# Softmax reciprocals through 32x32 VectorE transposes, a reordered first batch, and four FFN groups a step ahead of the third batch

## The chip, the cores and the metric

The kernel runs on one core of one Trainium2 chip. The metric is device microseconds (us) of an execution. Engines are named as in the profile: PE is TensorE, PEld its weight loads, DVE is VectorE, ACT is ScalarE, POOL is GpSimd, SP is SyncE.

## The reference

Eight batches of eight heads: causal attention of 576 queries over 16 "beacon" keys and 576 keys, then a gated feed-forward network over all 4608 rows. Cut to what matters:

```python
k_all = np.concatenate([beacon_k, k], axis=2); v_all = np.concatenate([beacon_v, v], axis=2)
scores = scale * np.matmul(q, k_all.transpose(0, 1, 3, 2))        # 8 x 8 x 576 x 592
scores = np.where(causal, -1e9, scores); scores -= scores.max(-1, keepdims=True)
a = np.exp(scores); a /= a.sum(-1, keepdims=True) + 1e-09
x = (a @ v_all) -> rows of 512                                     # 4608 x 512
out = (np.maximum(x @ w_gate, 0) * (x @ w_val)) @ w_out            # d_ff = 1536
```

## The kernel before

Batches are counted from 0 in the code and as first, second, third in the text. A batch has two groups of four heads. The queries of a group are cut into three chunks of 240, 256 and 80 columns. Per chunk TensorE multiplies the exponentials `e` with the values (into PSUM tile `ab`) and with a 32-column block of ones (into `os`). So each of the 32 rows of a head's block in `os` holds the same sum. VectorE takes the reciprocal, multiplies, and records the least and the most reciprocal ("notes"), which say at the end whether the sums were in range.

```python
class Chunk:
    def av(self):
        # ... PSUM tiles self.ab [P, 2, 256] and self.os [P, 256] are taken
        cq0, _, segs = CHUNKS[self.ci]
        order = sorted(segs, key=lambda x: x[0])
        for i, (kt, q0, n, _, _) in enumerate(order):
            # ... for three parts (two of values, one of ones), for four heads:
                    nc.tensor.matmul(o[:, q0 - cq0:q0 - cq0 + n], w, e[...], ...)
    def invert(self):
        n = CHUNKS[self.ci][1]
        self.r = nrm.tile([P, 256], FP32, name="r")
        nc.vector.reciprocal(self.r[:, :n], self.os[:, :n])
    def scale(self):   # xT = ab * r, on VectorE
    def note(self):    # least = min(least, r); most = max(most, r), on VectorE
```

The program interleaves attention steps of one batch with FFN groups of the batches before it. A FFN "up" group is 8 matmuls of 512 columns, a "down" group 12. A plan says how many groups each step carries. VectorE also makes the FFN product `hT` of each up group.

```python
ALONE = ((0, 3, 3, 2), (3, 3))       # FFN groups between first and second, second and third batch
plan = ([(0, i, 0) for i in range(STEPS)] + [(None, 0, n) for n in ALONE[0]]
        + [(1, i, 1) for i in range(STEPS)] + [(None, 0, n) for n in ALONE[1]]
        + [(b, i, 3.0 if b == 2 else 4.4) for b in range(2, B) for i in range(STEPS)]
        + [(None, 0, 4.5)])
```

In the first batch, tiles of q and k are cast, transposed on TensorE and moved out of PSUM as they land. Weight loads (`wg`, `wv`), the casting loads of the second batch (`hwide`) and `wo` are issued in this order:

```python
after(1, lambda: load_w(wg, moe_w_gate, 0, 512))
after(2, lambda: load_w(wv, moe_w_val, 0, 512))
after(3, lambda: load_w(wg, moe_w_gate, 512, 1024))
after(4, lambda: load_w(wv, moe_w_val, 512, 1024))
after(6, lambda: load_w(wg, moe_w_gate, 1024, 1536))
after(6, lambda: load_w(wv, moe_w_val, 1024, 1536))
after(6, lambda: load_second(0))                # hwide
# ...
after(s2 - 1, lambda: load_wo(0, 6)); after(s2, lambda: load_wo(6, 12))
```

## Time and profile before

| | before |
|---|---|
| median of the first three runs | 391.03 us (390.27 to 391.34) |
| first FFN matmul | 27.80 us |
| first score matmul of the third batch | 82.5 us |
| batch period from the fourth batch on | 40.6 us |
| TensorE busy | 370.4 us, 95% |
| VectorE busy | 204.8 us, of which the largest group of reciprocals 61.0 us |

The page of the profile begins with busy times (first line below), and its part 5 lists groups of instructions: line, engine, operation, output and input tiles, count, then busy time and mean ns, then the engine's idle time just before them and who ended it.

```profile
PE 370.4 (95%) x4239; PEld 188.1 (48%) x4296; DVE 204.8 (52%) x333; ACT 191.9 (49%) x269; POOL 125.9 (32%) x217
...
PE 85%; DMA 6%; POOL 4%; issue 2%; DVE 1%; ACT 1%; SPq 0%; DVEq 0%
...
L393 DVE RECIPROCAL r<-os 128x240 f32<-128x240 f32 (+2 forms) x45 | 61.0, 1355 | 39.6 <-PE os L385 39.5
...
L385 PE MATMUL os<-e,ones 128*32 128x240 bf16 (+4 forms) x660 | 31.7, 230 | 0.0
```

TensorE is the bottleneck. The sum matmuls (`os<-e,ones`, last line) are never waited for: their idle time is 0.0. The reciprocals are long, but stand beside the path.

Where TensorE does lose time is at the third batch. In the windows table the column after POOL is PEclk, the clock granted to TensorE as a share of full speed; then come the DMA share and GB/s.

```profile
82.50:86.00 3.50, 0.58 (x13) 0.42 (x12) 0.69 (x1) 0.97 (x1) 0.58 (x1) 0.87 0.55 153
86.00:88.00 2.00, 2.00 (x9) 0.70 (x9) 0.00 (x0) 0.00 (x0) 0.00 (x0) 0.50 0.78 177
```

TensorE waits 2.92 us for a transposing DMA (`qT<-half`) near 83 us, and then runs at half clock until about 91.5 us.

From the fourth batch on all is full. Two timelines of one place, TensorE and then VectorE (start, duration, engine, line, operation, count, and in brackets idle time before it and its releaser):

```profile
165.69 0.39 PE L385 MATMUL ab<-e,v 128*32 128x240 bf16 x8
165.90 0.28 PE L385 MATMUL os<-e,ones 128*32 128x240 bf16 x4
```

```profile
165.32 0.69 DVE L430 TENSOR_TENSOR hT<-g,f 128x512 bf16<-128x512 f32 x1 [1.18 <-PE f L428]
165.93 0.40 DVE L405 TENSOR_TENSOR least<-least,r 128x240 f32<-128x240 f32 x1
166.25 0.40 DVE L405 TENSOR_TENSOR most<-most,r 128x240 f32<-128x240 f32 x1
166.56 1.65 DVE L393 RECIPROCAL r<-os 128x240 f32<-128x240 f32 x1
```

The sums start at 165.90 us, 0.21 us behind the value matmuls. VectorE is then in the FFN product (to 166.0) and in two notes (to 166.6). Only behind those comes the reciprocal. Nothing on TensorE waits for that queue.

### The profile page before, as it was taken

What the parts mean: (1) busy time and instruction counts of PE and PEld (TensorE: products, weight loads), DVE (VectorE), ACT (ScalarE), POOL (GpSimd) and SP (SyncE); (2) the same over time, 40 slices, a digit from 0 to 9 for tenths busy, and PEclk for the clock granted to TensorE, in tenths of its full rate; (3) what the DMA queues carried; (4) which work ended last, traced back from release to release, by engine and by line L of the source; (5) the groups of instructions that cost most, each with busy time, mean ns of one, the idle gap of its engine ahead of it and who ended that gap; (6) DMA issues with size and microseconds to landing.
All of it is one profiled execution on the core that took longest, in us unless ns stands there. A gap on an engine that the chain in (4) does not pass through costs nothing.

```text
span 390.5 us, 10175 instructions
## 1 busy us (share of the span) xinstructions
PE 370.4 (95%) x4239; PEld 188.1 (48%) x4296; DVE 204.8 (52%) x333; ACT 191.9 (49%) x269; POOL 125.9 (32%) x217
## 2 busy tenths in 40 slices
PE   7779999969999999999999999999999999999995
PEld 3554455424555545445544545454544554444443
DVE  4877477524674565466546653666365654512420
ACT  4763494225745654465446545655455533323321
POOL 1796455324632543254224332335201100000000
PEclk9999999987999999999999999999999999999999
DMA  7899999858966983687357834786200010011002
GB/s 227 186 176 195 206 187 215 180 149 199 186 140 182 190 169 85 165 187 147 82 160 183 177 85 131 170 190 90 97 29 2 2 76 33 2 40 71 0 27 88
DMA packets 146788, 49.85 MB, mean 128 GB/s; under 512 B 133296, under 2 KB 142256, under 8 KB 146736
## 3 DMA queue, kind: packets, MB, share of 16 engines
q1 hardware_dynamic: 137680, 43.37, 47.1%
q0 software_dynamic: 9056, 5.77, 10.5%
q8 instruction: 35, 0.57, 0.7%
q14 instruction: 17, 0.14, 0.1%
HBM read 38.27 MB, written 9.44 MB: 122 GB/s over the span
## 4 chain that ended last, share of the span: by engine, by line
PE 85%; DMA 6%; POOL 4%; issue 2%; DVE 1%; ACT 1%; SPq 0%; DVEq 0%
PE f L438 24%; PE f L419 22%; PE s L428 11%; PE f L428 11%; PE s L336 6%; PE ab L385 6%; DMA wo<-in_moe_w_out_dram 3%; PE os L385 2%; DMA raw<-in_v_dram 1%; POOL e L352 1%; DMA wide<-in_k_dram 1%; PE f L282 1%; POOL v L245 1%; POOL wg L312 1%; POOL wv L312 1%
## 5 line engine op out<-in xcount | busy, mean ns | idle before, releaser
L344 ACT ACTIVATE e<-s 128x1024 bf16<-128x1024 f32 (+2 forms) x112 | 104.3, 966 | 23.9 <-PE s L336 23.8
L419 PE MATMUL f<-xT,wg 128*128 128x512 bf16 x407 | 110.8, 385 | 1.5 <-DVE hT L430 0.3
L422 ACT ACTIVATE g<-f 128x512 f32<-128x512 f32 x108 | 64.6, 598 | 89.7 <-PE f L419 82.9
L438 PE MATMUL f<-wo,hT 128*128 128x512 bf16 (+1 forms) x420 | 94.8, 373 | 2.9 <-issue 1.6
L352 POOL TENSOR_SCALAR_AFFINE_SELECT e<-e 128x512 bf16<-128x512 bf16 (+2 forms) x80 | 47.3, 603 | 153.0 <-ACT e L344 145.7
L393 DVE RECIPROCAL r<-os 128x240 f32<-128x240 f32 (+2 forms) x45 | 61.0, 1355 | 39.6 <-PE os L385 39.5
L430 DVE TENSOR_TENSOR hT<-g,f 128x512 bf16<-128x512 f32 x54 | 37.1, 687 | 61.7 <-PE f L428 55.8
L430 DVE TENSOR_TENSOR hT<-g,s 128x512 bf16<-128x512 f32 x54 | 37.1, 687 | 60.2 <-PE s L428 57.1
L428 PEld LDWEIGHTS <-wv 128*128 128x128 bf16 x432 | 42.6, 99 | 53.2 <-issue 3.7
L438 PEld LDWEIGHTS <-hT 128*128 128x128 bf16 x444 | 41.4, 98 | 47.2 <-issue 0.8
L419 PEld LDWEIGHTS <-wg 128*128 128x128 bf16 x432 | 40.3, 99 | 48.3 <-issue 2.8
L441 ACT COPY ob<-f 128x512 f32<-128x512 f32 (+1 forms) x37 | 21.3, 575 | 72.5 <-PE f L438 72.5
L428 PE MATMUL s<-xT,wv 128*128 128x512 bf16 x213 | 56.0, 384 | 0.1
L428 PE MATMUL f<-xT,wv 128*128 128x512 bf16 x213 | 55.4, 380 | 0.6 <-ACT qT L283 0.2
L249 POOL CAST half<-raw 128x512 bf16<-128x512 f32 (+2 forms) x60 | 36.3, 621 | 22.8 <-DMA raw<-in_q_dram 9.9
L385 PE MATMUL ab<-e,v 128*32 128x80 bf16 (+4 forms) x1320 | 38.7, 231 | 2.0 <-POOL e L352 1.0
L336 PE MATMUL s<-qT,kT 64*128 64x80 bf16 (+3 forms) x704 | 34.7, 231 | 5.4 <-DMA qT<-half 2.9
L336 PEld LDWEIGHTS <-kT 64*128 64x128 bf16 x704 | 20.4, 96 | 28.7 <-issue 26.0
L385 PE MATMUL os<-e,ones 128*32 128x240 bf16 (+4 forms) x660 | 31.7, 230 | 0.0
L385 PEld LDWEIGHTS <-v 128*32 128x32 bf16 (+1 forms) x1408 | 26.4, 97 | 10.5 <-issue 5.3
L245 POOL CAST v<-raw 128x512 bf16<-128x512 f32 (+1 forms) x40 | 26.1, 657 | 12.4 <-DMA raw<-in_v_dram 12.1
L398 DVE TENSOR_TENSOR xT<-ab,r 128x480 bf16<-128x480 f32 (+2 forms) x45 | 25.0, 555 | 1.0
(59 smaller groups left out, 130.9 us busy)
## 6 DMA issues: line engine op xcount, KB each, us to landing
out_dram<-ob SPq DMA_DIRECT2D x35, 256.0 KB, 2.3
raw<-in_v_dram SPq DMA_DIRECT2D x24, 256.0 KB, 4.9
raw<-in_q_dram SPq DMA_DIRECT2D x24, 256.0 KB, 4.3
raw<-in_k_dram SPq DMA_DIRECT2D x18, 256.0 KB, 4.2
raw<-in_v_dram SPq DMA_DIRECT2D x8, 224.0 KB, 3.5
wg<-in_moe_w_gate_dram POOLq DMA_DIRECT2D x6, 256.0 KB, 5.9
wv<-in_moe_w_val_dram POOLq DMA_DIRECT2D x6, 256.0 KB, 6.6
wo<-in_moe_w_out_dram POOLq DMA_DIRECT2D x2, 768.0 KB, 10.5
```

Source lines behind the costliest of these rows:

```text
L245: copy(self.v[:n, t].rearrange("p (h a d) -> p h a d", a=2, d=C), raw[:n].rearrange("p (h d a) -> p h a d", a=2, d=C))
L249: copy(h[:n], raw[:n])
L336: nc.tensor.matmul(self.s[:, a, c + j * n:c + (j + 1) * n], self.batch.kT[rows, 2 * g + j, kt * P:(kt + 1) * P], self.batch.qT[rows, 2 * g ...
L344: nc.scalar.activation(e[:, :k * 4 * n].rearrange("p (k a x) -> p a k x", k=k, a=2), self.s[:, :, :k * 2 * n].rearrange("p a (k x) -> p a ...
L352: nc.gpsimd.affine_select(out=cols[:, :, :m], in_=cols[:, :, :m], pattern=[[0, 4], [1, m]], compare_op=ALU.is_ge, fill=0.0, base=base, cha ...
L385: nc.tensor.matmul(o[:, q0 - cq0:q0 - cq0 + n], w, e[:kr, 2 * (hh % 2) + hh // 2], start=(i == 0 and part != 1), stop=(i == self.last), sk ...
L393: nc.vector.reciprocal(self.r[:, :n], self.os[:, :n])
L419: nc.tensor.matmul(g[:, :n], wg[:, ki, nf * P:(nf + 1) * P], x[:, ki], start=(ki == 0), stop=(ki == KM - 1))
L422: nc.scalar.activation(gs[:, :n], g[:, :n], AF.Relu)
L428: nc.tensor.matmul(u[:, :n], wv[:, ki, nf * P:(nf + 1) * P], x[:, ki], start=(ki == 0), stop=(ki == KM - 1))
L430: nc.vector.tensor_mul(self.h[:, nf, c0:c1], gs[:, :n], u[:, :n])
L438: nc.tensor.matmul(o[:, n], self.h[:, nf, ms * P:(ms + 1) * P], wo[:, nf, n], start=(nf == 0), stop=(nf == NF - 1))
```

## The change

The intent has three parts. They are called T, R and Q below.

- **T**: reciprocals through transposes. Since 32 rows hold the same sum, a 32x32 block transpose puts all sums of a block into each of its columns. One column in 32 is inverted, and a second transpose spreads the result back. A chunk of 240 or 80 columns isn't a whole number of blocks, so 16 pad columns of `os` are set to 1.0 ahead of the sums.
- **R**: the first batch's units and turns are reordered. (A unit is a score multiplication with its exponentials. A turn is a transpose on TensorE with the move of its result out of PSUM. The tails are the last 64 of the 576 rows of q and k.) One cast of q, its moves and the moves of the tails go from ACT to VectorE, and the tails are turned one step earlier; the casts of the tails were on VectorE already. There are fewer warm-up matmuls, and three of the weight loads are issued later.
- **Q**: four FFN groups instead of three in each of the two steps ahead of the third batch (quota 2.6 instead of 3.0 within it).

The core of the diff, cut:

```diff
 (T)
-            cq0, _, segs = CHUNKS[self.ci]
+            cq0, n, segs = CHUNKS[self.ci]
+            if n % C:
+                nc.vector.memset(self.os[:, n:n + C - n % C], 1.0)
             order = sorted(segs, key=lambda x: x[0])
 ...
-            n = CHUNKS[self.ci][1]
+            nb = -(-CHUNKS[self.ci][1] // C)
             self.r = nrm.tile([P, 256], FP32, name="r")
-            nc.vector.reciprocal(self.r[:, :n], self.os[:, :n])
+            few = nrm.tile([P, 8], FP32, name="few", bufs=2)
+            nc.vector.transpose(self.r[:, :nb * C], self.os[:, :nb * C])
+            nc.vector.reciprocal(few[:, :nb], self.r[:, :nb * C:C])
+            nc.vector.transpose(self.r[:, :nb * C].rearrange("p (b c) -> p b c", c=C),
+                                few[:, :nb].unsqueeze(2).to_broadcast([P, nb, C]))
 (Q)
-    ALONE = ((0, 3, 3, 2), (3, 3))
+    ALONE = ((0, 3, 3, 2), (4, 4))
-            + [(b, i, 3.0 if b == 2 else 4.4) for b in range(2, B) for i in range(STEPS)]
+            + [(b, i, 2.6 if b == 2 else 4.4) for b in range(2, B) for i in range(STEPS)]
 (R, cut: also UNITS_FIRST, HOLD, turn_next, turn_third, turn_last)
-            turn_tails(first, act, (ps[:, 0], ps[:, 1]))
+            turn_tails(first, dve, (ps[:, 0], ps[:, 1]))
-        after(2, lambda: load_w(wv, moe_w_val, 0, 512))
-        behind[3] = turn_first_tails
+        behind[2] = turn_first_tails
+        mid[3] = lambda: load_w(wv, moe_w_val, 0, 512)
-        after(3, lambda: load_w(wg, moe_w_gate, 512, 1024))
-        after(4, lambda: load_w(wv, moe_w_val, 512, 1024))
+        after(6, lambda: load_w(wg, moe_w_gate, 512, 1024))
+        after(6, lambda: load_w(wv, moe_w_val, 512, 1024))
```

## The prediction

> **What bounds the kernel now.** TensorE. Busy shares: PE 95% of 390.5 us, DVE 52%, ACT 49%, POOL 32%; the chain that ended last is PE for 85%. From the fourth batch on a batch takes 40.6 us (timeline: downs end at 161.5, 202.1, 242.7) with almost no PE gap, so nothing can be won there. What PE loses lies early. (a) First batch, 12 to 28 us: about 5 us of gaps while ACT runs 14 exponentials; the FFN starts at 27.8. (b) Third batch: PE idles 2.92 us at 83.0 for a transposing DMA (qT<-half, landing 85.8), and the windows table shows clock 0.50 until about 91.5, costing about 2.8 us more. The Trainium skill, "TensorE: Matmul & The Clock Gate", Part 1, says an idle window of about 3.4 us halves the clock; this trace agrees in kind (2.9 us idle, then matmuls at 0.43 instead of 0.22 us).
>
> **What changes.**
> 1. Reciprocal: 1.66 or 1.76 us (240, 256 columns), 0.66 (80), becomes two 32x32 transposes and a tiny reciprocal. Estimate from the 128x240 fp32 tensor ops of the trace (0.40 us): 0.40+0.12+0.40, about 0.95 us. DVE total falls by roughly 25 us. Off the path except in the first batch.
> 2. New: chunks of 240 and 80 columns get a VectorE memset of 16 PSUM columns before their sums. In the built program the first sum matmul waits for that memset (26 ones weight loads wait on VectorE, none before; the semaphore values name the memset). VectorE works in order, so the memset stands behind the FFN product (0.61) and two range notes (0.32 each for 240, 0.15 for 80). Placing it in the before timeline (product starts 165.32, memset could end near 166.7, sums were issued at 165.9): stalls of about 0.8, 0.55 and 0.8 us in chunks g0c0, g0c2, g1c0; g1c2 follows downs, none. About 2.2 us in each of batches 3 to 7 (counting from 0): +11 us. Batch 1 about +1, batch 2 +0.2.
> 3. First batch reordered: ACT loses a cast and tail copies (about 1.3 us), the second and third units start about 1 us earlier, but tail turns and memsets on VectorE gate PE. FFN start about 1.2 us earlier (0 to 3).
> 4. Two more FFN groups (2 x 1.73 us) before the third batch, quota 3.0 to 2.6: PE reaches it near 86, after the data; idle and half clock vanish: -5.7 us.
>
> **Sum.** 391.0 - 1.2 - 5.7 + 1.2 + 10.8 = about 396; I shade to 395, since stalls may prove shorter. Range 388.5 to 399.5. Chances: faster 0.04, within 2% 0.86, slower 0.10.
>
> **What would show it.** Batch period 40.6 to about 42.8 us; PE waits for "DVE os" (memset) at the sums, about 0.55 to 0.8 us, about 15 long ones; PE gaps in 100 to 320 us up from near zero to about 11 us. No wait over 1 us and no clock below 1 near 80 to 95. FFN start at 25 to 28. DVE busy down from 204.8 to about 180.
>
> **What would make it wrong.** The memset running earlier than I think, or PE absorbing the waits: then about 384 to 386. First batch faster by 4 us; but the wo weights (PE waited 0.56 us at 60.3) would give part back as a wait. Weight loads issued later stalling the FFN near 31 us. A clock drop from fewer warm-up matmuls: +3 us.

## The result, and the profile after

The kernel after took 410.02 us in the median (409.61 to 411.92, 4 runs), that of before 390.65 us (4 runs of the same rounds). The ratio is 1.0506, with a 95% interval of 1.0465 to 1.0548: slower by 19.4 us. A ratio is the mean time of one kernel's runs over that of the other's of the same rounds, so not quite the ratio of the medians quoted. Executions over 1.5% slower than the fastest of the same kernel are left out of the means. The range of the prediction (388.5 to 399.5) doesn't hold the result. It gave "slower" a chance of 0.10.

| | before | after |
|---|---|---|
| first FFN matmul | 27.80 us | 34.38 us |
| first score matmul of the third batch | 82.5 us | 94.6 us (3.5 of it are the two groups moved ahead) |
| first up group after the downs of the third batch | 120.8 us | 127.0 us |
| five batch periods | 120.8 to 323.4, 202.6 us | 127.0 to 342.9, 215.9 us |
| VectorE busy | 204.8 us | 192.9 us |

The lines of the page after that answer to those of before:

```profile
PE 380.6 (93%) x4293; PEld 188.1 (46%) x4293; DVE 192.9 (47%) x464; ACT 191.4 (47%) x266; POOL 126.7 (31%) x217
...
PE 70%; DMA 11%; DVE 8%; SPq 5%; POOL 2%; issue 1%; ACT 0%; DVEq 0%; POOLq 0%
...
L404 DVE STREAM_TRANSPOSE r<-os 128x256 f32<-128x256 f32 (+1 forms) x45 | 17.8, 395 | 79.5 <-PE os L393 79.5
...
L393 PE MATMUL os<-e,ones 128*32 128x240 bf16 (+4 forms) x660 | 32.7, 235 | 13.5 <-DVE os L382 13.4
```

The sum matmuls now have 13.5 us of idle time before them, and VectorE's `os` ended nearly all of it. That is line 382, the pad memset. VectorE's own share of the chain that ended last rose from 1% to 8%, although VectorE is busy for less time. The two timelines of the same place in a batch:

```profile
174.12 0.39 PE L393 MATMUL ab<-e,v 128*32 128x240 bf16 x8
175.22 0.29 PE L393 MATMUL os<-e,ones 128*32 128x240 bf16 x4 [0.70 <-DVE os L382]
```

```profile
173.76 0.69 DVE L444 TENSOR_TENSOR hT<-g,f 128x512 bf16<-128x512 f32 x1 [0.80 <-PE f L442]
174.36 0.40 DVE L419 TENSOR_TENSOR least<-least,r 128x240 f32<-128x240 f32 x1
174.68 0.40 DVE L419 TENSOR_TENSOR most<-most,r 128x240 f32<-128x240 f32 x1
175.09 0.07 DVE L382 MEMSET os<- 128x16 f32 x1
175.72 0.45 DVE L404 STREAM_TRANSPOSE r<-os 128x256 f32<-128x256 f32 x1 [0.56 <-PE os L393]
176.21 0.20 DVE L405 RECIPROCAL few<-r 128x8 f32<-128x8 f32 x1
176.44 0.45 DVE L406 STREAM_TRANSPOSE r<-few 128x256 f32<-128x256 f32 x1
```

The memset itself takes 0.07 us, but it stands behind the same FFN product and the same two notes as the reciprocal did before. TensorE has to wait for it in the middle of its work, since the program orders the sums behind the memset of the same tile. From the start of the value matmuls to the start of the sums it is 1.10 us, before it was 0.21. The Trainium skill, "PSUM — Partial Sum Buffer", section "Engine vs sequencer instructions", says that VectorE's queue is a strict FIFO and that matmuls run in program order. This trace agrees: nothing passed the memset on either engine, and 0.70 us was lost.

The transposes are fast. With 0.45, 0.20 and 0.45 us the three instructions take 1.1 us against 1.65 us.

In the first batch the same memset does more. TensorE and VectorE, the two short chunks at the end of the batch:

```profile
28.32 0.26 PE L393 MATMUL ab<-e,v 128*32 128x80 bf16 x8
30.00 0.22 PE L393 MATMUL os<-e,ones 128*32 128x80 bf16 x4 [1.43 <-DVE os L382]
...
32.00 0.33 PE L393 MATMUL s<-e,v 128*32 128x80 bf16 x8 [1.35 <-DVE s L382]
```

```profile
29.18 0.69 DVE L412 TENSOR_TENSOR xT<-f,r 128x512 bf16<-128x512 f32 x1
29.88 0.07 DVE L382 MEMSET os<- 128x16 f32 x1
30.70 0.28 DVE L404 STREAM_TRANSPOSE r<-os 128x96 f32<-128x96 f32 x1 [0.75 <-PE os L393]
...
31.54 0.32 DVE L412 TENSOR_TENSOR xT<-ab,r 128x160 bf16<-128x160 f32 x1
31.87 0.07 DVE L382 MEMSET s<- 128x16 f32 x1
```

Here each chunk's memset stands behind the transposes and the multiplication of the chunk before, and those wait for that chunk's sums. So TensorE and VectorE take turns, and TensorE waits 1.43 and 1.35 us. (The last chunk keeps values and sums in one tile `s`, so even its value matmuls wait.) In before these sums followed each other without VectorE in between: the last values began 0.03 us behind the sums of the chunk before.

```profile
26.02 0.22 PE L385 MATMUL os<-e,ones 80*32 80x80 bf16 x4
26.05 0.26 PE L385 MATMUL s<-e,v 128*32 128x80 bf16 x8
```

In the idle time of after the clock also fell, though no single wait was longer than 1.43 us, as its windows table shows (PEclk 0.50 and 0.74):

```profile
32.00:34.00 2.00, 2.00 (x63) 1.33 (x64) 0.69 (x3) 0.00 (x0) 2.00 (x3) 0.50 1.18 188
34.00:36.00 2.00, 2.00 (x8) 0.79 (x7) 0.37 (x2) 0.23 (x1) 2.00 (x4) 0.74 1.12 164
```

At the third batch the wait for `qT` at 83 us and its half clock are gone, as predicted. But TensorE waits elsewhere: 1.32 us for `wo` (0.56 before), twice about 0.55 us for masked exponentials of POOL, and 1.46 us for a later `qT` at 126 us.

### The profile page after: what moved, and what is told of

It is laid out like the page before. It is cut to its first block, busy times and chain, and to the rows that moved or that the text cites. A ratio compares the mean times of both kernels' runs of the same rounds, so it can differ in the third digit from the quotient of the medians.

```text
span 410.2 us, 10401 instructions
## 1 busy us (share of the span) xinstructions
PE 380.6 (93%) x4293; PEld 188.1 (46%) x4293; DVE 192.9 (47%) x464; ACT 191.4 (47%) x266; POOL 126.7 (31%) x217
## 3 DMA queue, kind: packets, MB, share of 16 engines
q0 software_dynamic: 9056, 5.77, 10.2%
## 4 chain that ended last, share of the span: by engine, by line
PE 70%; DMA 11%; DVE 8%; SPq 5%; POOL 2%; issue 1%; ACT 0%; DVEq 0%; POOLq 0%
PE f L452 20%; PE f L433 19%; PE s L442 11%; PE f L442 8%; DMA raw<-in_q_dram 5%; PE ab L393 4%; PE os L393 3%; DMA wo<-in_moe_w_out_dram 3%; PE s L342 3%; DVE hT L444 3%; SPq L236 3%; SPq L260 2%; DVE most L419 2%; DMA raw<-in_v_dram 1%; DMA qT<-half 1%
## 5 line engine op out<-in xcount | busy, mean ns | idle before, releaser
L452 PE MATMUL f<-wo,hT 128*128 128x512 bf16 (+1 forms) x444 | 96.9, 374 | 1.3 <-DMA wo<-in_moe_w_out_dram 1.3
L444 DVE TENSOR_TENSOR hT<-g,s 128x512 bf16<-128x512 f32 x60 | 41.2, 687 | 65.5 <-PE s L442 64.4
L442 PE MATMUL s<-xT,wv 128*128 128x512 bf16 x240 | 61.6, 379 | 0.0
L404 DVE STREAM_TRANSPOSE r<-os 128x256 f32<-128x256 f32 (+1 forms) x45 | 17.8, 395 | 79.5 <-PE os L393 79.5
L444 DVE TENSOR_TENSOR hT<-g,f 128x512 bf16<-128x512 f32 x48 | 33.1, 689 | 41.9 <-PE f L442 37.9
L442 PE MATMUL f<-xT,wv 128*128 128x512 bf16 x192 | 49.3, 379 | 0.2 <-ACT qT L289 0.2
L255 POOL CAST half<-raw 128x512 bf16<-128x512 f32 (+2 forms) x60 | 37.5, 639 | 29.4 <-DMA raw<-in_q_dram 11.2
L393 PE MATMUL os<-e,ones 128*32 128x240 bf16 (+4 forms) x660 | 32.7, 235 | 13.5 <-DVE os L382 13.4
L393 PE MATMUL ab<-e,v 128*32 128x80 bf16 (+4 forms) x1320 | 41.9, 236 | 1.1 <-POOL e L358 1.1
L251 POOL CAST v<-raw 128x512 bf16<-128x512 f32 (+1 forms) x40 | 26.6, 667 | 13.3 <-DMA raw<-in_v_dram 11.4
L393 PEld LDWEIGHTS <-ones 128*32 128x32 bf16 (+1 forms) x704 | 19.8, 100 | 19.6 <-DVE os L382 14.9
```

Source lines behind the costliest of these rows:

```text
L251: copy(self.v[:n, t].rearrange("p (h a d) -> p h a d", a=2, d=C), raw[:n].rearrange("p (h d a) -> p h a d", a=2, d=C))
L255: copy(h[:n], raw[:n])
L393: nc.tensor.matmul(o[:, q0 - cq0:q0 - cq0 + n], w, e[:kr, 2 * (hh % 2) + hh // 2], start=(i == 0 and part != 1), stop=(i == self.last), sk ...
L442: nc.tensor.matmul(u[:, :n], wv[:, ki, nf * P:(nf + 1) * P], x[:, ki], start=(ki == 0), stop=(ki == KM - 1))
L444: nc.vector.tensor_mul(self.h[:, nf, c0:c1], gs[:, :n], u[:, :n])
L452: nc.tensor.matmul(o[:, n], self.h[:, nf, ms * P:(ms + 1) * P], wo[:, nf, n], start=(nf == 0), stop=(nf == NF - 1))
```

## The experiments

Several effects of a few microseconds each can't be told apart by reading one trace, so the parts were run alone. All kernels gave correct results. For conversions, a ratio is turned into us as (ratio - 1) times 391.

Theory A: the place of the memset in VectorE's queue is the cause of the loss. Theory B: the transposes themselves, or the order of the first batch, hold VectorE or TensorE up.

### e1: after, with the memset behind the sums

```diff
-            if n % C:
-                nc.vector.memset(self.os[:, n:n + C - n % C], 1.0)
             # ... the matmuls ...
+            if width % C:
+                nc.vector.memset(self.os[:, width:width + C - width % C], 1.0)
```

The matmuls don't write the pad columns, so the memset may come behind them.

> The changed kernel with one edit: the VectorE memset of the 16 pad columns is issued after the sum matmuls, so that the transpose waits for it and TensorE does not. Theory A (TensorE waiting for the memset is the whole loss, in the steady batches and as a serial chain in the first batch): steady batch period back from 43.5 to 40.6 us, no wait of TensorE for a memset, FFN start back from 34.4 to 28 to 29.5 us, total 386 to 390. Rival B (the reordered first batch is slow by itself, because turns and casts went to VectorE): period 40.6 as well, but FFN start stays at 32 us or later, total 392 to 395.

Measured: 394.1 us (392.12 to 394.42), ratio 1.0085 [1.0034, 1.0137]. The batch period is 40.6 us again, and the first FFN matmul starts at 28.64 us. TensorE's waits from 90 to 340 us, first of e1, then of after (waiter, tile awaited; us in total, times, longest):

```profile
PE ab L391 <- POOL e L358: 0.4, 1, 0.4
```

```profile
PE os L393 <- DVE os L382: 10.9, 15, 1.1
```

Fifteen waits for the memset, 10.9 us, are gone. So about 16 of the 19.4 us are the memset's place, and the transposes may stay. The FFN's start is where theory A wanted it, but the total lies in the range that was given for rival B. So e1 is still not faster than before, though T and Q were to gain. Something else costs.

### e2: before with T alone, memset ahead

```diff
+            if n % C:
+                nc.vector.memset(self.os[:, n:n + C - n % C], 1.0)   # ahead of the sums
-            nc.vector.reciprocal(self.r[:, :n], self.os[:, :n])
+            nc.vector.transpose(...); nc.vector.reciprocal(few, ...); nc.vector.transpose(...)
```

> The kernel before with part 1 alone: transposed reciprocals and the memset ahead of the sums. Theory A: period 43.4 instead of 40.6 us (+13.5 in all), second batch +1 to 2, and FFN start later by 2 to 5 us than 27.8, because the sums of one chunk wait for the normalization of the one before; total 407 to 412. Rival B (the first batch's loss comes from the reordering): the same +13.5, FFN start within 1 us of 27.8, total 404 to 407.

Measured: 407.83 us (407.45 to 409.13), ratio 1.0442 [1.0385, 1.0499], +17.3 us. The first FFN matmul starts at 33.78 us, 6.0 us later than before, so the late start of the FFN does not need the reordering. The period is 43.1 us. TensorE's waits for the memset between 90 and 340 us add up to 10.2 us.

### e3: before with T alone, memset behind the sums

```diff
+            # behind the last sum matmul:
+            if width % C:
+                nc.vector.memset(self.os[:, width:width + C - width % C], 1.0)
-            nc.vector.reciprocal(self.r[:, :n], self.os[:, :n])
+            nc.vector.transpose(...); nc.vector.reciprocal(few, ...); nc.vector.transpose(...)
```

> The kernel before with the transposed reciprocals and the memset after the sums. Theory A: nothing waits for it, VectorE loses about 25 us of busy time off the path, the FFN starts 0 to 1 us earlier, total 389 to 391.5. Rival C (the longer train of dependent VectorE instructions costs by itself): total 393 or more, with TensorE waits for VectorE in the steady batches.

Measured: 391.77 us (391.05 to 392.54), ratio 1.0016 [0.9963, 1.007]; period 40.6 us, first FFN matmul at 27.57 us. The transposed reciprocals alone are worth nothing that this test can see, and cost nothing: they save VectorE time off the path. The time lies 0.3 us above the range expected and below the 393 us of rival C. Theory B falls for the transposes.

### e4: before with Q alone

```diff
-    ALONE = ((0, 3, 3, 2), (3, 3))
+    ALONE = ((0, 3, 3, 2), (4, 4))
-            ... 3.0 if b == 2 else 4.4
+            ... 2.6 if b == 2 else 4.4
```

> The kernel before with part 4 alone: four FFN groups in each of the two steps ahead of the third batch, quota 2.6 instead of 3.0. My prediction had -5.7 us for it: the 2.9 us wait for the third batch's data and the half clock after it both gone, total 385 to 386. The trace of after suggests that shorter steps in the third batch bring new waits (mask, the fourth batch's data: 1.5 us): total 386 to 389. If the wait for data moves instead of going away: 390 to 391.

Measured: 387.51 us (386.22 to 387.85), ratio 0.9916 [0.9866, 0.9967], -3.3 us. The third batch no longer waits for `qT`. The windows table of e4 has full clock where before had half, and a new hole two windows later, in which TensorE waits 1.02 us for a mask of POOL:

```profile
86.00:88.00 2.00, 2.00 (x11) 0.90 (x10) 0.42 (x1) 1.78 (x3) 1.11 (x2) 1.00 1.13 255
...
90.00:92.00 2.00, 0.98 (x23) 0.47 (x15) 0.42 (x1) 1.51 (x2) 2.00 (x4) 1.00 0.78 74
```

### e5 and e13: before with R alone

The kernel before with all of (R) of the diff above, plain reciprocals and three groups; its edit is the diff of the change without its parts (T) and (Q). It was run on two occasions, as e5 and as e13.

> Kernel before with the reordering of the first batch alone: plain reciprocals, three FFN groups in each step. Theory C (the reordering itself costs, by where it puts the weight loads, the hwide loads and the VectorE casts): the first FFN matmul comes 1 to 3 us later than the 27.8 us of before, hwide and wo are waited for longer (about 0.7 and 1.5 us against nearly 0 and 0.56), and because the first qk of the third batch comes later, part of the 2.92 us wait for qT goes; net 391 to 396 us. Rival (the reordering gains about 1 us as predicted, and e1's shortfall against e4 came from the late memset): FFN start by 27 us and 388 to 391 us.

> The kernel of e5 once more, on the same chip as e12, so that the worth of the late loads is read within one job: 1.010 to 1.018 as in e5, the difference to e12 between 2.7 and 4.7 us.

Measured: e5 396.33 us (392.78 to 398.34), ratio 1.0136 [1.009, 1.0181]; e13 396.28 us, ratio 1.0136 [1.0104, 1.0167]. The reordering costs 5.3 us, where I had predicted a gain of 1.2. The first FFN matmul starts at 29.79 us (e5) and 29.23 us (e13), against 27.80 in before. TensorE's waits from 40 to 100 us in e5, and in before:

```profile
PE s L342 <- DMA qT<-half: 2.9, 1, 2.9
PE f L444 <- DMA wo<-in_moe_w_out_dram: 2.2, 1, 2.2
...
PE s L288 <- DMA hwide<-in_k_dram: 0.7, 2, 0.4
PE f L288 <- DMA hwide<-in_q_dram: 0.5, 2, 0.3
```

```profile
PE s L336 <- DMA qT<-half: 2.9, 1, 2.9
PE f L438 <- DMA wo<-in_moe_w_out_dram: 0.6, 1, 0.6
```

What POOL issues after the weights is waited for longer. The third batch's `qT` lands later too: the wait for it ended at 92.98 us, in before at 85.90. So it didn't shrink, against the expectation of e5, though the third batch began seven microseconds later.

### e8: e1 with the weight loads at the steps of before

```diff
+        after(2, lambda: load_w(wv, moe_w_val, 0, 512))
-        mid[3] = lambda: load_w(wv, moe_w_val, 0, 512)
-        after(6, lambda: load_w(wg, moe_w_gate, 512, 1024))
-        after(6, lambda: load_w(wv, moe_w_val, 512, 1024))
+        after(3, lambda: load_w(wg, moe_w_gate, 512, 1024))
+        after(4, lambda: load_w(wv, moe_w_val, 512, 1024))
```

> e1 (kernel after with the memset behind the sums, 394.1 us, 1.0085) with the gate and value weight loads put back to the steps where before has them. Theory C1 (1.4 us of e1's loss against e4 is hwide that lands later, 0.7 us is wo that lands later, both since weight loads of the first batch were issued later): waits for hwide at 44 us (0.32 and 0.35) vanish, the wait for wo falls from 1.49 to about 0.8 us, and the time is 391 to 392.5 us. Rival (the loads are not it, the loss is the VectorE work of the tails and the clock): within 0.5 us of e1.

Measured: 389.02 us (388.41 to 389.82), ratio 0.9965 [0.9935, 0.9996]. It is 4.7 us better than e1 by the ratios, more than the 2.1 us that I had added up from the waits of e1's trace; e1's profiled run was its fastest and may show too little of them. The waits for `hwide` are gone, and that for `wo` fell from 1.49 to 1.01 us.

### e10 and e12: the late loads alone, and the reordering without them

e10 is the kernel before with the three loads at the late steps (the reverse of the diff above). e12 is e5 with the loads put back; e13 ran beside it on the same chip.

> Kernel before with nothing changed but the steps at which three gate and value weight loads are issued, put where the change puts them. Theory C1 (the late loads are the cost of the reordering: e8 gained 4.7 us by taking them back): 394 to 396 us, hwide waits near 40 us, the wait for wo up from 0.56 to 1.5 us or more, and the third batch's qT later still. Rival (they only hurt together with the other parts of the reordering): 390 to 392 us.

> The reordering alone (e5, 1.0136) with the gate and value weight loads at the steps of before. Its ratio to before is what the rest of the reordering is worth (order of the units, casts and moves on VectorE, fewer warm-up matmuls). If the late loads are 2.7 us of e5's 5.3 (e10) and the rest is a loss of its own: 1.005 to 1.007, about 393 us. If late loads are 4.7 us of it (e8 against e1): 1.001 to 1.003, about 391.5 us. If the rest gains 1.2 us, as predicted: 0.997.

Measured: e10 393.04 us, ratio 1.0068 [1.0037, 1.0099], +2.7 us, between the two expectations. Its trace has the longer waits of the first one, 1.4 us for `wo` and 0.9 for `hwide`. e12 391.77 us (390.87 to 396.13), ratio 1.0059 [1.0014, 1.0105], +2.3 us; against e13 of the same job the loads are worth 0.77% or 3.0 us. So the late loads are about 3 us of R's 5.3 (three comparisons give 2.7, 3.0 and 4.7), and the rest of R is about 2.3. A second comparison gives less for that rest: e8 and e9 (below) were of one job and differ in the reordering without its late loads alone, and e8 is 0.32% or 1.3 us slower (388.4 to 389.8 against 386.6 to 388.6 us). How late loads act is seen on POOL. Its lines in before, then in e13:

```profile
29.10 0.77 POOL L271 DMA_DIRECT2D hwide<-in_k_dram  x1
...
49.82 0.84 POOL L317 DMA_DIRECT2D wo<-in_moe_w_out_dram  x1
```

```profile
27.63 1.42 POOL L318 DMA_DIRECT2D wg<-in_moe_w_gate_dram  x2
...
33.31 0.77 POOL L277 DMA_DIRECT2D hwide<-in_k_dram  x1
...
54.94 0.84 POOL L323 DMA_DIRECT2D wo<-in_moe_w_out_dram  x1
```

Each weight issue holds POOL for 0.71 us (two in 1.42). The four issues that the change moved to step 6 push the `hwide` loads from 29.10 to 33.31 us and the second half of `wo` from 49.82 to 54.94 us. The Trainium skill, "DMA: Bandwidth & Descriptors", section "SWDGE vs HWDGE vs iDMA", says that descriptors of DMAs issued from GpSimd are computed in software on its cores; that agrees with a POOL that is busy for each of them here.

Of the rest of R, the trace of e12 shows one candidate: the tails, which R turns a step earlier. TensorE waits twice for their casts on VectorE, and before the second of these casts VectorE itself waited 1.21 us for the load of q (`raw<-in_q_dram`).

```profile
14.13 0.29 PE L311 MATMUL os<-ident,half 64*128 64x64 bf16 x4 [1.30 <-DVE half L303]
15.75 0.39 PE L311 MATMUL os<-ident,half 64*128 64x64 bf16 x4 [1.34 <-DVE half L303]
```

The granted clock then read 0.50 from 16 to 20 us. In before there is no such wait and the clock stays at 1.00, though its tail casts stand on VectorE too. But the two profiled executions differ in more than the kernel. In e12 groups of eight transposing matmuls took 0.41 us from 5.7 us on; in before they took 0.64 us until 12 us. In e5 and e13, which were like before in this, the same two waits are only 0.4 us each and the clock stays at 1.00. So part of e12's waits may show only that TensorE came early. No run put the tail turns alone back to their step or changed the warm-up alone, so this part is argued from the trace, not shown.

### e7: after with the memset ahead in the first batch only

```diff
-            if n % C:
+            if n % C and self.batch.b == 0:
                 nc.vector.memset(self.os[:, n:n + C - n % C], 1.0)
             # ... the matmuls ...
+            if width % C and self.batch.b:
+                nc.vector.memset(self.os[:, width:width + C - width % C], 1.0)
```

> Kernel after, with the pad memset ahead of the sum matmuls in the first batch only, and behind them in all others. Theory A (two separate costs of one cause: about 5 us in the first batch, about 2.9 us in each later batch): first FFN matmul near 34.4 us as in after, batch period 40.6 us as in e1, no wait for memset after 60 us, 397 to 401 us. Rival (the first batch's loss is made good later by waits it hides, or the later loss hangs on the first): FFN start 34.4 us but under 396 us, or a period above 41 us.

Measured: 396.04 us (393.64 to 396.81), ratio 1.0143 [1.0111, 1.0175]. That is 2.3 us above e1 and 14.2 us below after, by the ratios. The intervals leave some 2.5 us of play in the first of these. The expectation of 397 to 401 us was missed: FFN started at 33.47 us, 4.8 us later than in e1, but half of that came back. TensorE's waits of e7 from 10 to 90 us hold all the memset waits of the first batch, yet none for `wo` or `hwide`:

```profile
PE os L394 <- DVE os L383: 1.6, 2, 1.4
PE s L394 <- DVE s L383: 1.3, 1, 1.3
PE f L394 <- DVE f L383: 1.0, 1, 1.0
```

Here a TensorE that arrived later found the late loads landed: e1 waited 1.5 us for `wo` and 0.7 for `hwide`. So these two costs did not add in full. (The profiled run of e7 was its fastest, 393.64 us.)

### e9 and e11: looking for a better version

e9 is e4 with the transposed reciprocals and a late memset. e11 is e4 with the last pair of weight loads one step earlier:

```diff
-        after(6, lambda: load_w(wg, moe_w_gate, 1024, 1536))
-        after(6, lambda: load_w(wv, moe_w_val, 1024, 1536))
+        after(5, lambda: load_w(wg, moe_w_gate, 1024, 1536))
+        after(5, lambda: load_w(wv, moe_w_val, 1024, 1536))
```

> Kernel before with four FFN groups in each step (e4: 387.5 us, 0.9916) and the transposed reciprocals with the pad memset behind the sums (e3: 391.8 us, 1.0016). The best version that the parts suggest. If the transposes save only VectorE time off the critical path: 386 to 388 us, equal to e4. If they help once the qT wait is gone (VectorE free earlier): 384 to 386 us.

> e4 (kernel before with four FFN groups in each step, 387.5 us, 0.9916) with the last pair of gate and value loads issued one step earlier, so that hwide, v and wo follow earlier. If what holds for late loads holds the other way: the wait for wo falls from 0.76 us, 386 to 387 us. If the queue is already never waited for: no change within 0.5 us of e4.

Measured: e9 387.82 us (386.56 to 388.63), ratio 0.9933 [0.9903, 0.9963], the same as e4. The transposes gain nothing even with the wait for `qT` gone. e11 388.74 us, ratio 0.9948 [0.9925, 0.9971], no better, and outside both expectations. The wait for `wo` is gone in it, but earlier issues sit in front of a mask on POOL. POOL's lines, then TensorE's, which waits 2.55 us for that mask:

```profile
25.65 1.43 POOL L312 DMA_DIRECT2D wv<-in_moe_w_val_dram  x2
27.08 0.48 POOL L352 TENSOR_SCALAR_AFFINE_SELECT e<-e 128x320 bf16<-128x320 bf16 x1
```

```profile
27.62 0.26 PE L385 MATMUL s<-e,v 80*32 80x80 bf16 x8 [2.55 <-POOL e L352]
```

So the loads have a place between two harms, and before had it about right. The best version found is Q alone, e4, 0.8% faster than before and 5.6% faster than after; its interval overlaps those of e9 and e11.

## Why the prediction was wrong, point by point

The parts, run alone, add up to the whole: T +17.3 (e2), R +5.3 (e5), Q -3.3 (e4) make +19.3 us, and after was 19.4 us slower. Agreement to 0.1 us is luck, since each of these is uncertain by 1 to 2 us and e7 shows two costs that overlap. But it lets each term of the predicted sum be held against its own runs.

| term of the prediction | predicted | measured |
|---|---|---|
| steady batches, "+10.8", and batches 1 and 2, "+1.2" | +12.0 | +14.2 (after against e7) |
| first batch, "-1.2", with its memsets inside | -1.2 | +7.6 (R +5.3, and its memsets +2.3, e7 against e1) |
| third batch, "-5.7" | -5.7 | -3.3 (e4) |
| sum | +5.1 | +18.5 |

1. **The step that failed is the first batch: "First batch reordered ... FFN start about 1.2 us earlier (0 to 3)".** The FFN started 6.6 us later than in before, at 34.38 us. The stage is 8.8 of the 13.4 us by which the two sums differ. Two things are wrong in it.
   - I let the relief of ACT decide the FFN's start and wrote that "tail turns and memsets on VectorE gate PE" without adding it up. In the trace the memsets made a chain in which TensorE and VectorE take turns; it held TensorE by 1.43 and 1.35 us at the last two chunks and let the clock fall (after, 30 to 36 us). I had worked the memset's wait out only for the steady batches, where an `hT` product and two notes stand ahead of it. In the first batch a whole chunk's reciprocal and product stand there.
   - I looked for the price of the late weight loads at the FFN ("stalling the FFN near 31 us") and not at what is issued behind them by the same engine. The FFN never waited for `wg`. `hwide`, `wo` and with them the whole second batch came later: 3.0 us (e12 against e13).
2. **The memset's wait in steady batches was right in kind and in size; a smaller term was missing.** Predicted were waits of 0.8, 0.55 and 0.8 us, of "DVE os", three in each batch, and none in the fourth chunk. Measured were 0.70, 0.50 and 0.70 us, or 1.14 in some batches, 10.9 us in all against 10.8. That these sums agree so well is luck: at 0.70, 0.50 and 0.70 us everywhere they would be 9.5, and the longer waits of point 3, which I had not foreseen, make up the rest. And five periods grew by 13.3 us. The other part goes with the cut of the matmul group in two. In the timeline above the sums start 0.89 us later relative to the value matmuls than in before, of which only 0.70 is shown as idle: 0.19 us more for each of 15 waits, about 2.8 us, an estimate from those lines. The Trainium skill, "TensorE: Matmul & The Clock Gate", section "Single matmul latency", gives about 175 ns for the drain of a single matmul, beside the time for its columns. The 0.18 to 0.19 us here are near that; that the drain is the cause is inferred.
3. **The 1.14 us waits** come when a note takes 0.84 instead of 0.40 us; in the trace of after POOL runs casts at that time (198.6 us). The Trainium skill, "SBUF — State Buffer", section "Who interferes with whom", says that a VectorE instruction with two SBUF inputs contends with a GpSimd instruction that reads SBUF, as these are. The trace agrees in kind, but not for every note: the one at 198.31 us took 0.40 us though POOL was in a cast. No run took the casts away, so this cause is not shown.
4. **The third batch: mechanism right, size too large.** The wait for `qT` and the half clock vanished. The term counted all of 2.92 + 2.8 us from one profile. In e4 1.02 us of it came back as a wait for POOL's mask at 91 us, where before had none. And the profile that I read was of one of the longer runs: before was measured between 388.6 and 392.7 us, and its profiled run took 392.2. How the rest of the difference arises isn't known.
5. **The VectorE saving was overstated and didn't matter.** Predicted was about 180 us busy; measured 192.9. With T alone it is 191.8 (e3): the transposes take 0.45 us and not 0.40, the tiny reciprocal 0.20 and not 0.12. R's cast and moves add 0.8 to 1.9 us (e13, e5). That it lay "off the path" was right: e3 and e9 show no gain at all.
6. **The chances.** Two of my "what would make it wrong" points were of the right sort (late weight loads, the clock), but both stood as side remarks and didn't widen the range. The range of 11 us assumed that the errors of the terms would mostly cancel; here all three came out on the dear side.

What stays open: which piece of R beyond the loads costs the last 1.3 to 2.3 us (earlier tail turns, moves on VectorE, the order of the units, or fewer warm-ups), and how much of the spread of 1.4 to 5.6 us between runs of one kernel comes from the first 12 us, in which some profiled executions have fast transposing matmuls (0.41 us for eight: e4, e10, e11, e12) and others slow ones (0.64 us: before, after, e1, e5, e13). e4 and before have the same first batch but differ in this, and e4's FFN starts 1.1 us earlier; so its trace shows not only Q.

## What to carry to other kernels

An instruction that takes 0.07 us costs what stands ahead of it on its engine's queue, once a bottleneck engine waits for it. Before adding one, write down what it follows there at every place, the first stage and the last chunks too, and put it where nobody waits: behind the sums it was free. When loads are moved, follow everything that the same engine issues behind them, not only the loads' own readers. And run the parts of a change alone: here one part gained 3.3 us, one gained nothing, and two placements, of a memset and of three loads, lost about 20.

## What the Trainium skill lacked or had wrong

- "VectorE: DVE Perf Modes", "The three transpose paths": its table has one time for VectorE's transpose, 128x128 bf16 (311 ns). Here an fp32 transpose took 0.45 us for 128x256 and 0.28 us for 128x96, from PSUM or from a broadcast source alike.
- The same page gives no time for a reciprocal. Here 1.76, 1.65 and 0.66 us for 256, 240 and 80 columns of fp32, and 0.20 us for 8.
- "TensorE: Matmul & The Clock Gate", Part 1, lets the array warm up after about 3.4 us of sustained work. In e1 TensorE was busy for 1.86 to 1.90 us of each 2 us from 6 to 12 us by the profile's modelled ends, yet groups of eight transposing matmuls still took 0.64 us at 13.8 us, against 0.41 us in e12 from 5.7 us on; the granted clock in the windows table reads 1.00 in both until 14 us. The cause isn't known.
- "DMA: Bandwidth & Descriptors", "Anatomy of one DMA — SWDGE (gpsimd) path", says how long such a DMA takes, but has no figure for how long its issue holds GpSimd. Here 0.71 us for each 256 KB weight load, 0.74 to 0.77 us for most casting loads of 128 KB, and 0.82 to 0.84 us for one of 768 KB.
- No page warns that a pad memset of an accumulation tile joins VectorE's queue to TensorE's. Here there were 15 such waits of 0.50 to 1.15 us, and five batches took 13.3 us longer.
